# Input rows of the last two column groups loaded straight into the kept token rows, with every job and ring buffer of the first stage placed anew

## The chip, the cores and the metric

The kernel runs on one core of one Trainium2 chip. The metric is the device time of one execution in microseconds (us). A core has five engines with an instruction stream each: TensorE (PE, matmuls; PEld is its weight load), VectorE (DVE), ScalarE (ACT), GpSimd (POOL) and SyncE (SP, which here only issues DMA transfers). The streams run side by side, each in its own order, and wait for one another through semaphores. A DMA issue that has to wait holds up everything behind it in the stream that issues it.

## The reference

A block of 2048 tokens with 640 columns: a layer norm with modulation, a state-space convolution over the sequence per column, a second norm, and a bilinear gated network, each with a gated residual. Cut to what matters:

```python
mod = (silu(c) @ w_mod).reshape(1, 6, 1, -1)          # sa, ca, ga, sb, cb, gb
h = layernorm(x) * (1 + ca) + sa
K = einsum("dn,dnl,dn->dl", C, exp(dt * A * l), dt * B).real   # a filter of 2048 taps per column
y = irfft(rfft(pad(h)) * rfft(pad(K)))[:L] + h * Dskip
x = x + ga * y
h = layernorm(x) * (1 + cb) + sb
x = x + gb * (((h @ w_gate) * (h @ w_up)) @ w_down)
```

All is computed in float32; the large products of the second stage are split into high and low parts in a reduced format and summed from three products.

## The kernel before

**First stage, the convolution (about the first 465 us).** The 640 columns are five groups of 128 (`db` = 0 to 4), the tokens are four blocks of 512 (`c` or `q` = 0 to 3). The filter of each column is generated in 40 pieces (`n`), each in three parts: ACT takes sines, POOL forms phases and exponentials, DVE multiplies them (QtA, PtA, PtB, QtB), PE sums them into the bank `kg` (L825, L840). Around this loop of 144 steps lie the other jobs, each a Python generator that is emitted in segments:

- `u_stats`, `u_hm`: row statistics and normalised rows, stored to `hm`;
- `u_modr`, `u_fold`: modulation vectors on PE, folded on DVE (L392 to L404);
- `u_seeds`: the start values of each group's filter;
- `u_k`, `u_pre`, `u_g`, `u_c`: transforms of filter and rows, their product (DVE L946 to L956), and the way back, whose result goes to `WD` (store L972; by SP during the filter loop, by ACT behind it);
- `u_d(db, c)`: the end of a column group for a token block. It loads its part of `WD` (L980, into a buffer `TVa` or `TVb`) and the input rows (L982, into `xsa` or `xsb`), sums on PE (L988), adds the input rows on DVE (L992 or L995) and stores to `x2d` (L996).

**The order.** It is written out: the table `SCHED` holds a number for every segment of every job, and `due` emits a segment when the loop reaches that number (20 units are one step of the loop, two calls of `due`). Engines then run in this order. A second table, `SLOT`, names for each use of a ring buffer the letter (`a`, `b`, `c`) that it takes; a use waits until the last user of that letter is done.

**The kept rows.** The second stage begins with token blocks 0 and 1, whose rows stay in SBUF as `XB[0]`, `XB[1]` (`xb0`, `xb1`), in memory that the filter's pools give up after the last filter piece. Columns of groups 0 to 2 are read back from `x2d` (`rows`, L1384). For groups 3 and 4 (`db >= NB - 2`) and blocks 0 and 1 (`c < 2`) `u_d` writes its sum straight to `XB` (L992) and stores it to `x2d` as well, where it is read later for the residual.

**Change-over.** The last jobs are `u_d(3, 2)` and `u_d(3, 3)`, then `u_d(4, c)` in the order 0, 3, 1, 2, with `u_d(0, 2)` before the last. `warm` (L1196) puts 30 and then 4 filler matmuls on PE. `u_head` takes statistics of block 0 (L1156), normalises and transposes it (L1186) and begins the first products (L1223) as soon as `u_d(4, 0)` is done; block 1 follows after `u_d(4, 1)`. While this goes on, weight tiles (`wga`, L1021) are loaded by SP and split.

**Second stage (505 us to the end).** The gated network, half of the tokens at a time, on PE almost without a gap.

Of the kernel before, what the change touches and what calls it, by code (L numbers as in the profile page):

```python
# [14 lines left out]
OP = mybir.AluOpType  # L15
# [3 lines left out]
P = 128  # L19
# [12 lines left out]
    ml=(47, -888, -934),  # L32
    mr=(((138, 140), (110, 111)), ((2, 74), (4, 83)), ((0, 27), (-862, 18))),
    st=(
        (48, 91),
        (69, 100),
        (71, 101),
        (-948, 5),
        (-1006, 0),
        (-965, 89),  # L40
        (-1010, -969),
        (-868, 34),
        (-938, -874),
        (-918, 0),
        (-1003, -929),
        (-947, -909),
        (-919, -868),
        (34, 63),
        (37, 69),
        (-912, 0),  # L50
    ),
    hm=(
        (10, 220),
        (302, 416),
        (-1002, 172),
        (-999, 389),
        (-1010, 182),
        (-961, 147),
        (59, 100),
        (123, 173),  # L60
        (246, 310),
        (290, 372),
        (162, 252),
        (121, 180),
        (210, 293),
        (297, 381),
        (391, 486),
        (473, 556),
    ),
    rstd=(124, 87),  # L70
    tab=(367, 828),
    fo=(162, 162, 208, 238),
    e0=(4, 158),
    ds=(483, 468, 275, 262),
    mc=((87, 192, 194, 200, 210), (153, 286, 303, 326, 337), (270, 359, 369)),
    q=(
# [4 lines left out]
    ),  # L81
    pre=(
# [5 lines left out]
    ),  # L88
    c=(
# [4 lines left out]
        (  # L94
            (2433, 2608, 2608, 2648, 2679, 2703),
            (2425, 2484, 2537, 2554, 2645, 2677),
            (2477, 2493, 2636, 2656, 2680, 2719),
            (2387, 2439, 2532, 2545, 2620, 2633),
# [8 lines left out]
    ),  # L107
    k=(
        (392, 464),
        (371, 384),  # L110
        (474, 512),
        (494, 503),
        (622, 637),
        (592, 599),
        (710, 710),
        (607, 639),
        (640, 677),
        (652, 660),
        (831, 865),
        (797, 803),  # L120
        (973, 990),
        (941, 961),
        (1060, 1060),
        (1060, 1060),
        (1125, 1152),
        (1353, 1363),
        (1274, 1275),
        (1390, 1425),
        (1482, 1495),
        (1506, 1519),  # L130
        (1576, 1590),
        (1524, 1542),
        (1757, 1758),
        (1791, 1791),
        (1747, 1747),
        (1720, 1720),
        (2005, 2019),
        (1893, 1909),
        (2048, 2049),
        (2020, 2031),  # L140
        (2083, 2095),
        (2218, 2252),
        (2287, 2298),
        (2350, 2355),
        (2328, 2328),
        (2344, 2352),
        (2461, 2497),
        (2497, 2510),
    ),
    low=(168, 419, 677, 899, 1101, 1385, 1631, 1857, 2075),  # L150
    w=(2478, 2613, 2684, 2668, 2879, 2879),
    wl=(2590, 2441),
    wm=(2732, 2755),
    h=(2709, 2738, 2775, 2811, 2843, 2843, 2857, 2875),
    g=(
# [1736 lines left out]
```

## Time and profile before

| What | Value |
|---|---|
| median of three runs | 964.95 us |
| lowest and highest | 959.68, 966.23 us |
| the profiled execution, its own time | 962.34 us |
| its span, first to last instruction | 960.6 us |
| mean granted TensorE clock in it | 0.989 |
| DMA: read and written in HBM | 124.22 MB, 62.59 MB |

All readings come from the one profiled execution; its time is 1.74 us over its span and 2.61 us under the median. In rows of the timeline the first number is the start in us from the span's beginning, the second the duration, then the engine (with a q behind its name: a DMA issue in that engine's stream), the line of the kernel, the operation, written tile <- read tiles, and in brackets the idle time before it and what ended it. Ring letters stand at the end of a tile's name (`TVa`, `xsb`).

### The profile page before, as it was taken

What the parts mean: (1) busy time and instruction counts of PE and PEld (TensorE: products, weight loads), DVE (VectorE), ACT (ScalarE), POOL (GpSimd) and SP (SyncE); (2) the same over time, 40 slices, a digit from 0 to 9 for tenths busy, and PEclk for the clock granted to TensorE, in tenths of its full rate; (3) what the DMA queues carried; (4) which work ended last, traced back from release to release, by engine and by line L of the source; (5) the groups of instructions that cost most, each with busy time, mean ns of one, the idle gap of its engine ahead of it and who ended that gap; (6) DMA issues with size and microseconds to landing.
All of it is one profiled execution on the core that took longest, in us unless ns stands there. A gap on an engine that the chain in (4) does not pass through costs nothing.

```text
span 960.6 us, 27559 instructions
## 1 busy us (share of the span) xinstructions
PE 892.6 (93%) x11646; PEld 734.0 (76%) x11646; DVE 705.6 (73%) x1250; ACT 580.5 (60%) x1016; POOL 471.2 (49%) x369
## 2 busy tenths in 40 slices
PE   1898787999899899998889999999999999999998
PEld 1675555878776677887558888889999788888997
DVE  8977888878888986767688555557585766569952
ACT  6989999887988977763276333234463543435430
POOL 3998997986699668750041345320013323231110
PEclk9989999999999999999999999999999999999999
DMA  7876546435267646547894675435536576758875
GB/s 238 324 243 242 186 131 199 146 108 153 78 207 197 187 124 194 184 128 228 277 308 152 192 246 192 165 140 172 200 120 196 171 238 208 244 172 289 253 231 189
DMA packets 158819, 188.59 MB, mean 196 GB/s; under 512 B 9828, under 2 KB 128360, under 8 KB 157544
## 3 DMA queue, kind: packets, MB, share of 16 engines
q1 hardware_dynamic: 149480, 155.51, 50.3%
q0 software_dynamic: 4752, 21.63, 7.8%
q10 hardware_dynamic: 4464, 9.70, 2.7%
q8 instruction: 91, 1.49, 0.6%
q14 instruction: 32, 0.26, 0.1%
HBM read 124.22 MB, written 62.59 MB: 194 GB/s over the span
## 4 chain that ended last, share of the span: by engine, by line
PE 61%; ACT 12%; issue 10%; DVE 7%; POOL 5%; DMA 4%; SPq 0%; POOLq 0%; DVEq 0%; ACTq 0%
PE pa L1095 19%; PE psg L1095 9%; PE pa L1527 7%; PE kg L825 3%; PE kg L840 2%; PE psfa L907 2%; PE psfb L967 2%; PE psfb L907 2%; ACT L235 2%; PE psfc L967 1%; PE psfc L907 1%; PE psfa L967 1%; PE psfc L886 1%; ACT trb L235 1%; ACT tra L235 1%
## 5 line engine op out<-in xcount | busy, mean ns | idle before, releaser
L1072 POOL TENSOR_TENSOR tf<-wur,wgb 128x256 f32<-128x256 f32 x23 | 17.5, 760 | 241.5 <-DVE wtl L1043 193.2
L729 POOL TENSOR_TENSOR EQ<-LQ,RH 128x1536 f32<-128x1536 f32 x40 | 114.8, 2870 | 5.3 <-DVE QtB L785 5.3
L1043 DVE TENSOR_TENSOR wtl<-tf,wth 128x256 fp32r<-128x256 f32 (+1 forms) x72 | 37.0, 516 | 59.2 <-ACT wth L235 59.2
L729 POOL TENSOR_TENSOR Phb<-LH,DH 128x1536 int32<-128x1536 int32 x21 | 60.3, 2871 | 32.6 <-ACT trb L235 19.3
L729 POOL TENSOR_TENSOR EP<-LP,RH 128x768 f32<-128x768 f32 x40 | 61.9, 1547 | 1.7 <-ACT RH L235 1.7
L729 POOL TENSOR_TENSOR Pha<-LH,DH 128x1536 int32<-128x1536 int32 (+1 forms) x20 | 54.1, 2703 | 9.2 <-ACT trb L235 8.5
L1527 PE MATMUL pa<-wsg,sh 128*128 128x384 f32 (+1 forms) x304 | 58.1, 309 | 0.0
L840 PEld LDWEIGHTS kg<-QtB,PtB 64*32 64x32 f32 x2560 | 38.3, 108 | 13.4 <-issue 6.9
L1043 DVE TENSOR_TENSOR wsg<-wga,wsg 128x640 fp32r<-128x640 f32 x36 | 35.5, 988 | 14.8 <-ACT wsg L235 14.8
L840 PE MATMUL kg<-QtB,PtB 64*32 64x64 f32 x2560 | 44.6, 219 | 1.8 <-DVE QtB L785 1.8
L1527 PEld LDWEIGHTS pa<-wsg,sh 128*128 128x128 f32 x304 | 45.4, 188 | 0.0
L1566 POOL DMA_DIRECT2D wsg<-wdc x21 | 11.2, 532 | 66.6 <-PE pa L1579 35.7
L235 ACT ACTIVATE sh<-a 128x512 fp32r<-128x512 f32 x55 | 33.3, 626 | 13.9 <-PE psg L1579 6.2
L1043 DVE TENSOR_TENSOR sl<-a,sh 128x512 fp32r<-128x512 f32 x55 | 38.0, 710 | 3.9 <-ACT sh L235 3.9
L235 ACT ACTIVATE wsg<-wga 128x640 fp32r<-128x640 f32 x36 | 26.2, 731 | 23.7 <-PE pa L1527 12.6
L1095 PE MATMUL pa<-hh,wsg 128*128 128x512 f32 x150 | 40.0, 393 | 0.0
L235 ACT ACTIVATE a<-pa 128x512 f32<-128x512 f32 x12 | 7.2, 596 | 49.9 <-PE pa L1095 49.9
L235 ACT ACTIVATE s<-pa 128x512 f32<-128x512 f32 x12 | 7.2, 598 | 49.2 <-PE pa L1095 47.0
L235 ACT ACT_TABLE_LOAD x25 | 32.1, 1283 | 7.2 <-DMA pta<-A_A_re 4.2
L784 DVE TENSOR_TENSOR QtA<-trb,EQ 128x1024 f32<-128x1024 f32 x22 | 26.8, 1216 | 11.9 <-POOL EQ L729 4.4
L235 ACT ACTIVATE wth<-tf 128x256 fp32r<-128x256 f32 (+1 forms) x72 | 32.4, 481 | 4.5 <-DVE tf L1073 1.8
L1527 PE MATMUL pa<-wsg,sl 128*128 128x384 f32 (+1 forms) x152 | 34.5, 308 | 0.0
(672 smaller groups left out, 3230.0 us busy)
## 6 DMA issues: line engine op xcount, KB each, us to landing
wsg<-wdc POOLq DMA_DIRECT2D x21, 640.0 KB, 5.1
wgb<-B_w_gate SPq DMA_DIRECT2D x24, 320.0 KB, 4.1
wur<-B_w_up SPq DMA_DIRECT2D x24, 320.0 KB, 5.6
wsd<-wsg SPq DMA_DIRECT2D x12, 640.0 KB, 3.7
wga<-wdg SPq DMA_DIRECT2D x12, 640.0 KB, 3.9
wsg<-wsd POOLq DMA_DIRECT2D x12, 640.0 KB, 4.8
wdc<-xb SPq DMA_DIRECT2D x21, 320.0 KB, 4.5
TVb<-WD SPq DMA_DIRECT2D x26, 256.0 KB, 3.5
```

Source lines behind the costliest of these rows:

```text
L235: return S.activation(o, i, f, **kw)
L729: G.tensor_tensor(o.rearrange("p x (h l) -> p x h l", l=8), lo.unsqueeze(2).to_broadcast([P, rows, nh, 8]), hi.unsqueeze(3).to_broadcast([ ...
L784: return [lambda: V.tensor_tensor(Qt[:, :, :, 0:32], tr[:, :, :, ::-1], e[:, :, 0:32].unsqueeze(1).to_broadcast([P, 2, R, 32]), op=OP.mult ...
L825: PE.matmul(kg[j * 32 : j * 32 + 32, dd, :], PtA[:, c, dl * 4 + j, :], QtA[:, c, dl * 4 + j, :], start=dd == 0 and c == 0, stop=False, til ...
L840: PE.matmul(kg[j * 32 : j * 32 + 32, dd, :], PtB[lo : lo + 64, c, r, :], QtB[lo : lo + 64, c, r, :], start=False, stop=dd == 7 and c == 1, ...
L907: PE.matmul(r[c][par * 64 : par * 64 + 64, i, :], t_tw[:, k0 + k, c, :], src[:, k, :], start=True, stop=True, tile_position=(0, par * 64))
L967: PE.matmul(r[par][:, i], t_ti[lo : lo + 64, qd * 4 + i, c, :], y[lo : lo + 64, i, :], start=k == 0, stop=k == len(x) - 1, tile_position=( ...
L1043: V.tensor_tensor(lo, v, hi, op=OP.subtract)
L1072: E.tensor_tensor(t[:, 0:2], u[:, 0:2], g[:, 0:2], op=OP.subtract)
L1095: PE.matmul(ps, w[a][:, k], x[b][:, l], start=first and n == 0 and m == 0, stop=n == 2 and m == len(ks) - 1, skip_group_check=True)
L1527: PE.matmul(AC[tb][t][c], x[:, ts], w[:, cs], start=st, stop=f == NF - 1 and n == 2 and (c == 0 or t % 2 == 1))
L1566: G.dma_start(WD[q], wdc[:, q // 3, q % 3])
```

## The change

Four `u_d` jobs, groups 3 and 4 for blocks 0 and 1, no longer load input rows into the ring `xs`. Instead one transfer per block (`kept_l`, placed by a new entry `xl`) brings the 256 columns of both groups from the input straight to `XB[c]`, as soon as that memory is free; the add is made in place. The store to `x2d` is made once per block, of both groups together, by whichever of the two jobs comes second. The ring `xs` has 16 uses in place of 20. Every number in `SCHED` and most letters in `SLOT` are new.

```diff
 SCHED = dict(
-    ml=(47, -888, -934),
+    ml=(31, 2, -977),
...
-    fo=(162, 162, 208, 238),
+    fo=(155, 185, 229, 232),
...
-        ((2736, 2744, 2754), (2780, 2829, 2831), (2836, 2874, 2875), (2749, 2762, 2784)),
+        ((2704, 2713, 2734), (2715, 2775, 2775), (2776, 2869, 2879), (2713, 2753, 2753)),
...
+    xl=(2453, 2441),
 )
...
     def u_d(db, c):
...
-        xs = ring(fp, [P, 4, P], "xs")
-        SY.dma_start(xs, xin[:, 4 * c : 4 * c + 4, db * P : db * P + P])
-        yield
         d0 = slice(db * P, db * P + P)
+        kept = db >= NB - 2 and c < 2
+        if not kept:
+            xs = ring(fp, [P, 4, P], "xs")
+            SY.dma_start(xs, xin[:, 4 * c : 4 * c + 4, d0])
+        yield
         ps = ring(PF[-1], [P, 4, P], "psf")
...
         mark("d", c)
-        if db >= NB - 2 and c < 2:
-            V.tensor_tensor(XB[c][:, :, d0], ps, xs, op=OP.add)
+        if kept:
+            need(1, "xl", c)
             xs = XB[c][:, :, d0]
-        else:
-            V.tensor_tensor(xs, ps, xs, op=OP.add)
+        V.tensor_tensor(xs, ps, xs, op=OP.add)
+        if kept:
+            mark("kept", c)
+            if done["kept", c] < 2:
+                return
+            d0, xs = LAST, XB[c][:, :, LAST]
         SY.dma_start(x2d[:, 4 * c : 4 * c + 4, d0], xs)
...
+    LAST = slice((NB - 2) * P, NB * P)
...
+            def kept_l(tb):
+                SY.dma_start(XB[tb][:, :, LAST], xin[:, 4 * tb : 4 * tb + 4, LAST])
+                mark("xl", tb)
+
             for j in range(2):
                 XB[j] = mk(f"xb{j}", [P, 4, D])
+                at(T0["xl"][j : j + 1], once(kept_l), j)
                 at(T0["wl"][j : j + 1], once(rows), j)
```

Three places show what the new numbers do to the order. The first is SP's stream where the memory of the filter's pools comes free. `TV.. <-WD` and `xs.. <-A_u` are the loads of a `u_d`, `xb1`, `xb0` the kept rows, `gha<-FH` a load for `u_g(4, 0)`, `wga` weights of the second stage. Before:

```order
L921 DMA gha_6827<-FH_3434 128x1024
L980 DMA TVa_6849<-WD_4349 128x4x128 x2
L982 DMA xsa_6852<-A_u 128x4x128
L980 DMA TVb_7001<-WD_4349 128x4x128 x2
L982 DMA xsa_7004<-A_u 128x4x128
L1384 DMA xb1_7000<-x2d_62 128x4x384
L996 DMA x2d_62<-xb1_7000 128x4x128
L1021 DMA wga0_7060<-B_w_gate 128x5x256
L996 DMA x2d_62<-xb0_6999 128x4x128
L1384 DMA xb0_6999<-x2d_62 128x4x384
L1021 DMA wga1_7182<-B_w_gate 128x5x256
L980 DMA TVb_7247<-WD_4349 128x4x128 x2
```

And now:

```order
L981 DMA TVa_6847<-WD_4351 128x4x128 x2
L981 DMA TVb_6988<-WD_4351 128x4x128 x2
L1395 DMA xb1_7010<-A_u 128x4x256
L1395 DMA xb0_7009<-A_u 128x4x256
L922 DMA gha_7075<-FH_4018 128x1024
L1029 DMA wga0_7107<-B_w_gate 128x5x256
L981 DMA TVb_7109<-WD_4351 128x4x128 x2
L986 DMA xsb_7112<-A_u 128x4x128
L1392 DMA xb1_7010<-x2d_62 128x4x384
L1392 DMA xb0_7009<-x2d_62 128x4x384
L1029 DMA wga1_7265<-B_w_gate 128x5x256
L981 DMA TVa_7274<-WD_4351 128x4x128 x2
```

The load `gha<-FH` has moved from ahead of the group-3 jobs to behind the two new loads, two stores are gone, and the loads of `u_d(3, 2)` (the last row before; `TVb_7109`, `xsb_7112` now) stand ahead of the read-back of the kept rows.

The second place follows directly in SP's stream: the change-over. `WD_3435` before and `WD_4019` now are group 4. Before:

```order
L980 DMA TVb_7247<-WD_4349 128x4x128 x2
L982 DMA xsb_7250<-A_u 128x4x128
L980 DMA TVa_7258<-WD_4349 128x4x128 x2
L982 DMA xsa_7261<-A_u 128x4x128
L1021 DMA wga0_7266<-B_w_gate 128x5x256
L996 DMA x2d_62<-xsa_7261 128x4x128
L996 DMA x2d_62<-xsb_7250 128x4x128
L980 DMA TVb_7366<-WD_3435 128x4x128 x2
L982 DMA xsb_7369<-A_u 128x4x128
L980 DMA TVa_7410<-WD_3435 128x4x128 x2
L982 DMA xsa_7413<-A_u 128x4x128
L996 DMA x2d_62<-xb0_6999 128x4x128
```

And now:

```order
L981 DMA TVa_7274<-WD_4351 128x4x128 x2
L986 DMA xsa_7277<-A_u 128x4x128
L1029 DMA wga0_7286<-B_w_gate 128x5x256
L1003 DMA x2d_62<-xsa_7277 128x4x128
L981 DMA TVb_7363<-WD_4019 128x4x128 x2
L981 DMA TVa_7402<-WD_4019 128x4x128 x2
L986 DMA xsa_7405<-A_u 128x4x128
L981 DMA TVb_7407<-WD_4019 128x4x128 x2
L1003 DMA x2d_62<-xsb_7112 128x4x128
L1003 DMA x2d_62<-xb0_7009 128x4x256
```

The load of group 4's block 0 (`TVb_7366`, now `TVb_7363`) has one store ahead of it in place of two, and no load of input rows beside it.

The third place is DVE early in the first stage, at the end of a filter piece and the fold of the modulation (`mcol`, `dt2`, `dcol`; `PtB`, `QtB`, `QtA` are products for the filter). Before:

```order
L402 SCALAR_TENSOR_TENSOR mcol_137<-psfb_679,mcol_137 128x1
L403 TENSOR_TENSOR dt2_98<-psfb_679,dt2_98 128x4
L404 TENSOR_TENSOR dcol_138<-psfb_679,dcol_138 128x4
L810 TENSOR_TENSOR PtB_670<-trb_672,EP0_142 128x512
L784 TENSOR_TENSOR QtB_671<-trb_672,EQ0_140 128x16x32
L785 TENSOR_TENSOR QtB_671<-trb_672,EQ0_140 128x16x32
L784 TENSOR_TENSOR QtA_753<-tra_756,EQ1_141 128x32x32
```

And now:

```order
L585 TENSOR_TENSOR DH1_155<-psfc_687,shl_78 128x4x24x2
L811 TENSOR_TENSOR PtB_676<-trb_678,EP0_142 128x512
L785 TENSOR_TENSOR QtB_677<-trb_678,EQ0_140 128x16x32
L786 TENSOR_TENSOR QtB_677<-trb_678,EQ0_140 128x16x32
L393 TENSOR_SCALAR psfa_656<-psfa_656 128x5
L394 TENSOR_SCALAR mcol_137<-psfa_656 128x5
L395 TENSOR_TENSOR psfa_656<-psfa_656,mcol_137 128x5
```

The three products have moved from behind the fold's 13 small operations to ahead of them.

More of the change, by code (lines that the diff above doesn't have):

```diff
@@ L70 @@
-    rstd=(124, 87),
-    tab=(367, 828),
-    fo=(162, 162, 208, 238),
-    e0=(4, 158),
-    ds=(483, 468, 275, 262),
-    mc=((87, 192, 194, 200, 210), (153, 286, 303, 326, 337), (270, 359, 369)),
-    q=(
[4 rows of a table removed]
+    ml=(31, 2, -977),
+    mr=(((138, 143), (111, 123)), ((51, 71), (73, 90)), ((15, 18), (26, 35))),
+    st=(
+        (81, 101),
+        (90, 113),
+        (80, 115),
+        (-1010, 9),
+        (-868, 3),
+        (-908, 82),
+        (-1008, -967),
+        (6, 27),
+        (-956, -888),
+        (0, 3),
+        (-1008, -936),
+        (-965, -926),
+        (-964, 0),
+        (17, 29),
+        (30, 64),
+        (0, 7),
+    ),
@@ new lines @@
+    hm=(
+        (132, 397),
+        (444, 478),
+        (160, 173),
+        (-928, 211),
+        (110, 203),
+        (37, 155),
+        (76, 110),
+        (160, 210),
+        (230, 306),
+        (190, 299),
+        (217, 299),
+        (136, 163),
+        (314, 379),
+        (318, 379),
+        (384, 459),
+        (524, 568),
+    ),
+    rstd=(129, 84),
+    tab=(361, 785),
+    fo=(155, 185, 229, 232),
+    e0=(0, 166),
+    ds=(514, 285, 379, 342),
+    mc=((94, 198, 208, 210, 212), (178, 287, 305, 317, 338), (254, 334, 375)),
@@ L81 @@
+    q=(
[4 rows of a table added]
     ),
     pre=(
[5 rows of a table removed]
-    ),
-    c=(
[4 rows of a table removed]
-        (
[L95 to L98, printed above, removed]
[5 rows of a table added]
+    ),
+    c=(
[4 rows of a table added]
+        (
+            (2430, 2529, 2529, 2529, 2586, 2624),
+            (2426, 2426, 2487, 2494, 2584, 2621),
+            (2457, 2466, 2550, 2602, 2624, 2669),
+            (2382, 2420, 2476, 2476, 2546, 2613),
         ),
@@ L101 @@
     d=(
[5 rows of a table removed]
-    ),
-    k=(
[L109 to L148, printed above, removed]
-    ),
@@ L150 @@
[L150 to L154, printed above, removed]
-    g=(
[5 rows of a table removed]
[5 rows of a table added]
+    ),
+    k=(
+        (380, 499),
+        (365, 392),
+        (457, 508),
+        (483, 514),
+        (588, 609),
+        (574, 593),
+        (698, 706),
+        (609, 624),
+        (656, 684),
+        (664, 679),
+        (844, 868),
+        (795, 802),
+        (999, 1002),
+        (980, 980),
+        (1041, 1046),
+        (1046, 1083),
+        (1122, 1141),
+        (1341, 1341),
+        (1257, 1262),
+        (1399, 1426),
+        (1515, 1542),
+        (1484, 1498),
+        (1563, 1571),
+        (1519, 1534),
+        (1741, 1742),
+        (1780, 1789),
+        (1742, 1759),
+        (1721, 1721),
+        (2063, 2078),
+        (1896, 1917),
+        (2006, 2015),
+        (2028, 2039),
+        (2087, 2095),
+        (2200, 2229),
+        (2243, 2256),
+        (2255, 2277),
+        (2326, 2339),
+        (2349, 2360),
+        (2449, 2453),
+        (2463, 2475),
+    ),
@@ L161 @@
+    low=(173, 418, 671, 891, 1110, 1385, 1595, 1841, 2116),
+    w=(2479, 2608, 2615, 2621, 2879, 2879),
+    wl=(2556, 2523),
+    wm=(2709, 2721),
+    h=(2662, 2670, 2744, 2774, 2814, 2839, 2863, 2875),
+    g=(
[5 rows of a table added]
     ),
+    xl=(2453, 2441),
 )
 SLOT = dict(
-    Kt="abababbaabababbababa",
-    Ph="ababababababababababbbabababababaaababbb",
-    PtA="abababababababababababababababbabaababba",
-    TV="baabababaabbaabbbabbaababbaababbaabbabbaababab",
-    W="abbbbbabababbbbabbaabbaba",
-    f16="abababa",
@@ L177 @@
-    "a",
-    xs="aabababbabaaabababab",
+    Kt="abababbaabababbababb",
+    Ph="ababababababababababababababababaabababb",
+    PtA="abaaababababbbababababababababaabbababaa",
+    TV="baababaabaababababbbaabababaaababaabaaaaababab",
+    W="babaabaabaaaaabbabaabbaba",
+    f16="abababa",
+    gh="acabcacbcaccbacbcbbabcabcabccaabcabacba",
+    hf="aaccbcacbabacabcbabccabaaabbcbacaccabcabcaccabcacbabcbacbabaaacbb",
+    psf="bcbccbaaaacacbacbacabcacbbcaacbacacabcacbcbbabcabcbacbbcbcbcabcabcbaabccabacacbbacbacbacbacabababcabcabcabbcabcabcacacaa"
@@ L179 @@
+    "cbcbaacbacbacbabcabcbacacbacacbabcabcbacbbcabcbbabccbacabcbacbacbacbabaccabacbabcacbacbacababcbabccbacbacbacacabcacbcabc"
+    "acabbcabcacbacbacacbacbacbcbacabcabc",
+    tr="ababababababbbabababababababababababababababaaabababbbababababaaababababababababbbababababababababababaababbbbabababaaba"
+    "b",
+    xs="bababbababbbaaab",
 )
@@ L980, in u_d @@
             SY.dma_start(Vt[:, h], v[:, h, 4 * c : 4 * c + 4])
-        xs = ring(fp, [P, 4, P], "xs")
-        SY.dma_start(xs, xin[:, 4 * c : 4 * c + 4, db * P : db * P + P])
+        d0 = slice(db * P, db * P + P)
+        kept = db >= NB - 2 and c < 2
+        if not kept:
+            xs = ring(fp, [P, 4, P], "xs")
+            SY.dma_start(xs, xin[:, 4 * c : 4 * c + 4, d0])
         yield
-        d0 = slice(db * P, db * P + P)
         ps = ring(PF[-1], [P, 4, P], "psf")
```

39 lines of the change are left out of this document (removed), and 44 rows, old and new, of tables (c, d, g, pre).

## The prediction, made before the changed kernel ran

> **What bounds the kernel now.** I read the page first (share of each engine, then the 40 slices), then a table by stretches of the span, then the chain of work that ended last, and last the timeline of each engine between 425 and 505 us, where the edited jobs stand.
>
> ```profile
> span 960.6 us, 27559 instructions
> PE 892.6 (93%) x11646; PEld 734.0 (76%) x11646; DVE 705.6 (73%) x1250; ACT 580.5 (60%) x1016; POOL 471.2 (49%) x369
> ```
>
> The averages hide stages with different limits, so the next table cuts the span: start, three parts of the first stage, its last columns (437 to 465), the change-over to the second stage (465 to 505), and the second stage. After the two times come PE, PEld, DVE, ACT and POOL busy, then clock, DMA share and GB/s.
>
> ```profile
> 0.00:48.00 48.00, 26.14 (x275) 18.39 (x276) 43.81 (x129) 36.68 (x53) 30.73 (x37) 1.00 0.83 281
> 48.00:168.00 120.00, 99.68 (x2071) 71.77 (x2071) 98.53 (x161) 112.63 (x187) 106.82 (x67) 0.93 0.61 200
> 168.00:312.00 144.00, 138.76 (x3396) 108.95 (x3396) 119.03 (x165) 122.02 (x211) 120.62 (x69) 1.00 0.50 148
> 312.00:437.00 125.00, 118.06 (x2888) 94.99 (x2880) 98.99 (x132) 95.91 (x163) 86.86 (x46) 0.99 0.54 163
> 437.00:465.00 28.00, 23.68 (x496) 20.37 (x484) 18.74 (x39) 8.96 (x16) 0.00 (x0) 1.00 0.81 249
> 465.00:505.00 40.00, 35.54 (x180) 21.23 (x181) 30.02 (x88) 20.47 (x38) 9.78 (x15) 1.00 0.91 295
> 505.00:960.60 455.60, 450.72 (x2380) 398.28 (x2378) 296.46 (x539) 183.87 (x353) 116.43 (x138) 1.00 0.61 199
> ```
>
> From 505 us on PE is busy 450.72 of 455.60 us and the change touches nothing there: what is gained before 505 reaches the end one for one, and what is lost too. Up to 437 us the busiest engine of each stretch (DVE, ACT, PE, PE) stands idle for 4.19 + 7.37 + 5.24 + 6.94 = 23.7 us in all: no order of the same work gains more than that there. From 465 to 505 the DMA engines are busy for 0.91 of the time, and PE's 35.54 us are partly filler (30 warm-up matmuls). This is the place the edit is about.
>
> **The change-over, as it runs now.** The chain shows two loads of input rows on it:
>
> ```profile
> 461.72 7.58 DMA xsa<-A_u
> 474.75 2.96 DMA xsb<-A_u
> ```
>
> The timeline tells what they hold. First SP's issues: the eight loads of the last jobs of column group 3 and the first of group 4 (column group 4, token block 0 is the job that the second stage waits for).
>
> ```profile
> 457.34 1.02 SPq L980 DMA_DIRECT2D TVb<-WD  x2
> 458.42 0.96 SPq L982 DMA_DIRECT2D xsb<-A_u  x1
> 459.82 1.80 SPq L980 DMA_DIRECT2D TVa<-WD  x2
> 461.72 1.10 SPq L982 DMA_DIRECT2D xsa<-A_u  x1
> 472.14 0.91 SPq L980 DMA_DIRECT2D TVb<-WD  x2
> 474.75 0.37 SPq L982 DMA_DIRECT2D xsb<-A_u  x1
> ```
>
> Then PE, ACT and DVE, with what ended their idle time in brackets:
>
> ```profile
> 466.46 1.42 PE L988 MATMUL psfc<-TVa,ct 64*32 64x512 f32 x6 [1.76 <-DMA TVa<-WD]
> 469.10 7.09 PE L1196 MATMUL psg<-wsg 128*128 128x512 f32 x30
> 476.12 1.32 PE L988 MATMUL psfa<-TVb,ct 64*32 64x512 f32 x8
> 460.40 0.33 ACTq L972 DMA_DIRECT2D WD<-Wa  x1
> 466.55 0.60 ACT L235 ACTIVATE Wa<-psfb 128x512 f32<-128x512 f32 x1 [3.47 <-DMA WD<-Wa]
> 467.67 0.33 ACTq L972 DMA_DIRECT2D WD<-Wa  x1
> 477.80 0.69 DVE L992 TENSOR_TENSOR xb<-psfa,xsb 128x512 f32<-128x512 f32 x1 [0.94 <-DMA xsb<-A_u]
> ```
>
> The reader is to see that three things end close together. PE waits 1.76 us for TVa, then does the two group-3 jobs, then 30 warm-up matmuls to 476.19, and starts the job for block 0 at 476.12, with no gap. The TVb load for that job goes out at 472.14, because the last store of its data was issued at 467.67, after ACT had waited 3.47 us for the earlier store from the same buffer. And DVE's add at 477.80 waits for the input rows, though its matmul ended at 476.12 + 1.32 = 477.44. So the ring of input rows is directly worth only 0.36 us here. The 7.58 us on the chain is mostly covered: behind it stands the store (467.67 to 472.14), and behind both PE's warm-up.
>
> **The parts.** (a) The four 256 KB loads and four stores of the kept jobs become two and two of twice the size; PE's and DVE's instructions stay the same in number and shape. For the add of block 0 the wait for input rows goes: 477.80 - 477.44 = 0.36 us, bounds 0 and -0.94 (the whole idle time before it). I take -0.36.
>
> (b) The group-3 job of token block 2 is loaded before c's last jobs instead of at 457.34. Together with (a) that takes 0.5 MB (TVb and xsb) out of the queue just ahead of TVa, xsa and ACT's store. TVa's own issue does not move: it waits for the same DVE product in the same ring slot. At best TVa lands before PE is ready, which gives the 1.76 us; at worst nothing. The store that took from 460.40 to 466.5 shrinks too. How far it can is seen from one that met less traffic:
>
> ```profile
> 367.02 3.41 DMA WD<-Wb
> ```
>
> At 3.41 us it would be over before PE's results are ready at 466.46 - 1.76 = 464.7; ACT's copy then starts 1.8 us earlier, and the store, the TVb load and PE's job can follow by as much. Bounds -1.76 (PE's warm-up run is then the limit) and 0. I take -1.76, because 0.5 MB at the 295 GB/s of this stretch is 1.8 us of transfer. [...]
>
> (c) Block 1's group-3 add moves on DVE from ahead of a group-4 product to behind all of them.
>
> ```profile
> 440.50 0.69 DVE L992 TENSOR_TENSOR xb<-psfa,xsa 128x512 f32<-128x512 f32 x1 [3.52 <-PE psfa L988]
> 444.23 0.69 DVE L946 TENSOR_TENSOR TVa<-psfb,f16a 128x512 f32<-128x512 f32 x1 [0.73 <-PE psfb L907]
> 437.35 1.15 PE L907 MATMUL psfb<-f16b,t_tw 128*64 128x64 f32 x32
> 446.91 1.10 PE L907 MATMUL psfb<-f16b,t_tw 128*64 128x64 f32 x32
> ```
>
> DVE's 3.52 us wait goes, and one product starts some 2.6 us earlier. But the next one (444.23) waits for PE, which runs without a gap from 437.35 to 446.91, in the same order as after the change. Cost 0, hidden by PE; if that cover were gone it would be worth up to -2.6.
>
> (d) The two new loads wait for memory that the kernel-generation pools give up, and SP stands there until the last product has been read; behind them now stands a group-4 load (gha<-FH).
>
> ```profile
> 436.39 1.03 PE kg L840 x64
> 429.83 0.37 SPq L921 DMA_DIRECT2D gha<-FH  x1
> 449.78 0.44 PE L907 MATMUL psfc<-gha,t_tw 128*64 128x128 f32 x4 [1.55 <-DVE ghc L956]
> ```
>
> The last kernel matmul ends at 437.42, so the loads go out at about 438, and gha at about 439 instead of 429.83. PE needs it at about 448, and until 449.78 a PSUM bank would hold it anyway. In the queue are two times 512 KB and gha's 512 KB: 1.5 MB at the 249 GB/s of this stretch is 6.3 us, landing near 445.5. Cost 0, with some 4 us in hand; the upper bound is the second rival.
>
> (e) All other moves. Apart from ring letters, 24 of PE's 2918 rows, 44 of DVE's 1116, 66 of ACT's 1012 and 7 of POOL's 336 stand elsewhere; SP's are shuffled most (76 of 365). Two places show the sign.
>
> ```profile
> 57.32 0.17 DVE L392 TENSOR_SCALAR psfb<-psfb 128x5 f32<-128x5 f32 x1 [2.59 <-PE psfb L387]
> 59.31 0.69 DVE L810 TENSOR_TENSOR PtB<-trb,EP 128x512 f32<-128x512 f32 x1
> 60.51 0.68 DVE L785 TENSOR_TENSOR QtB<-trb,EQ 128x512 f32<-128x512 f32 x1
> 42.28 0.82 DVE L484 BATCH_NORM_STATS2 st<-Wb 128x6 f32<-128x320 f32 x2
> 42.45 0.20 POOL L1281 TENSOR_TENSOR ry<-rs 128x10 f32<-128x10 f32 x1 [1.67 <-DVE rs L1280]
> ```
>
> At the fold three products (59.31 to 61.19, 1.9 us) move ahead of the fold's vector work, into the 2.59 us in which DVE waits for PE: -1.9 for DVE. At 42 us the statistics of one more row (42.28, 0.82 us, with its aggregate about 1.0) move ahead of the reciprocal that POOL waits for: +1.0 for POOL. The net of the two is -0.9. The remaining moves are bounded by -23.7 (the idle time above) and, taking an equal amount of new waits, +23.7; the moved share of ACT's rows (66 of 1012) of 23.7 us is 1.5 us either way, and I take 0 for them.
>
> **Sum**, against the profiled execution's own time of 962.34 us (its span is 960.6): 962.34 - 0.36 - 1.76 + 0 + 0 - 0.9 = 959.3 us. That execution lies 2.6 us under the median of the three runs (964.95; lowest 959.68), so part of the offset returns: I forecast 960 us.
>
> **Rivals.**
> 1. The change-over doesn't shrink: TVa and the store are as late as before, since wga (640 KB) and the stores keep the DMA engines at 0.91 without the half megabyte. For it: two of the three limits must move together. Against: the 7.58 us. Time 962.34 - 0.36 - 0.9 = 961.1, or some 962 as a median.
> 2. Slower: SP held at the new loads, as in (d). It decides when gha lands after 449.78. If the two new loads took as long as the four they replace, one after another, with the median landing times of
>
> ```profile
> xsa<-A_u SPq DMA_DIRECT2D x11, 256.0 KB, 4.8
> ghc<-FH SPq DMA_DIRECT2D x6, 512.0 KB, 4.9
> ```
>
> gha would land at 438 + 4 x 4.8 + 4.9 = 462.1, which is 12.3 us late: 971.6 us. Against: loads overlap in this trace (four issued within 6 us at 457), and the new rows are twice as long.
> 3. The first stage wins back a good part of its 23.7 us idle, since most moved groups on DVE put kernel products ahead of work that can wait. A quarter of it, 6 us: 953.3 us. Against: PE's order hardly changes, PE is 96% busy from 168 to 312, and between 48 and 168 ACT and POOL pass the lead to each other, so that DVE's gains end in their queues.
>
> **How the numbers follow.** The forecast's case (change-over shrinks, rest neutral) gets 0.48, rival 1 gets 0.20, rival 3 gets 0.20, rival 2 or another loss of that kind in the moved SP queue 0.12. A measurement of this kernel can't tell changes under about 1% (9.6 us) from none; faster is under 955.3 and slower above 974.6. Rival 3 gives nearly all of faster (0.20). Rival 2 at 971.6 lies within 1%; only its worse part, with losses elsewhere in the moved SP queue, lies beyond: slower 0.08, same 0.72. The range 951 to 968 takes in the forecast's case, rival 1, most of rival 3 and the cheap half of rival 2.
>
> **What would show it.** In the profile after: no wait of the block-0 add for A_u rows; TVa's wait on PE under 1 us; the last WD store issued before 466.5 (less what the first stage shifts); the warm-up run ending where the block-0 job starts; gha landing before PE asks for it. The forecast is wrong if the second stage starts (PE's unbroken run) more than 8 us away from 505 less the shift at 437, or if the last kernel matmul moves from 437.4 by more than 6 us.

## The result: 0.6% slower, where no change or a small gain was forecast

| | before | after |
|---|---|---|
| median of 16 runs each | 962.86 us | 968.77 us |
| lowest and highest | 959.68, 968.88 | 966.58, 972.09 |
| ratio, 95% interval | | 1.0057 (1.0039 to 1.0074) |
| the profiled execution, its span | 962.34, 960.6 us | 969.30, 967.5 us |
| mean granted clock in it | 0.989 | 0.979 |

Beside later experiments the unedited changed kernel ran again: 970.02 us, 1.0088 (1.0058 to 1.0119). So by the two ratios it is slower by 5.5 to 8.5 us. Both intervals lie above 1, although the prediction held that nothing under about 1% can be told here. The time lies outside the range that was given (951 to 968), and the change has the other sign.

The page of the changed kernel:

```profile
span 967.5 us, 27557 instructions
PE 897.5 (93%) x11646; PEld 738.2 (76%) x11646; DVE 703.8 (73%) x1250; ACT 581.5 (60%) x1016; POOL 472.0 (49%) x369
```

The same stretches as in the prediction's table (two times, PE, PEld, DVE, ACT, POOL busy, clock, DMA share, GB/s):

```profile
48.00:168.00 120.00, 98.33 (x1968) 71.34 (x1966) 95.21 (x159) 109.41 (x181) 107.70 (x67) 0.90 0.61 201
168.00:312.00 144.00, 139.02 (x3307) 108.90 (x3307) 119.19 (x165) 121.87 (x210) 116.06 (x67) 0.99 0.48 141
465.00:505.00 40.00, 34.34 (x216) 21.61 (x216) 28.25 (x86) 16.96 (x31) 9.66 (x15) 0.91 0.83 253
505.00:967.50 462.50, 456.40 (x2409) 402.95 (x2407) 299.52 (x546) 190.44 (x365) 117.13 (x139) 1.00 0.61 201
```

Between 48 and 168 us ACT did 3.2 us less work in the same 120 us than before (109.41 against 112.63), at a lower PE clock (0.90, before 0.93). So time is lost there already. Three rows fix where the rest goes: the last kernel matmul, the start of the warm-up run, and the first transposes of block 1 (`pa<-ident,xb`), which open PE's unbroken run. Before, these stood at 436.39 (ending 437.42), 469.10 and 497.42. After:

```profile
441.57 1.10 PE L841 MATMUL kg<-QtB,PtB 64*32 64x64 f32 x64
474.81 7.10 PE L1204 MATMUL psg<-wsg 128*128 128x512 f32 x30
503.84 1.47 PE L1194 MATMUL pa<-ident,xb 128*128 128x128 f32 x12
```

From 437.42 to 442.67 the first stage ends 5.25 us later; from there to the warm-up 32.14 us in place of 31.68; from there to the transposes 29.03 in place of 28.32. Behind them 463.69 us against 463.15. The sum is 5.25 + 0.46 + 0.71 + 0.54 = 6.96, the difference of the profiled times.

**Where the 5.25 us come in.** Following the kernel matmuls (those that write `kg`) by their number, the two traces are 0.8 us apart at 65 us and 4.6 us at 110 us; from 126 to 437 us the distance is mostly between 4.5 and 6.6. On POOL the row that shows it is the start of the next group's phases (`D<-ptb`), which waits for a chain of small PE and ACT jobs. Before, then after:

```profile
98.05 0.74 POOL L667 TENSOR_TENSOR D<-ptb 128x96 int32<-128x96 int32 x2 [3.04 <-issue]
```

```profile
102.87 0.74 POOL L668 TENSOR_TENSOR D<-ptb 128x96 int32<-128x96 int32 x2 [2.81 <-DVE ptb L663]
```

The rows ahead of it on PE, before: the first of the fold's transposes, the row products behind them, the products of the last modulation rows.

```profile
51.95 1.27 PE L387 MATMUL psfb<-ident,TVb 1*128 1x1 f32 x10 [1.24 <-ACT TVb L235]
59.08 4.00 PE L368 MATMUL psfa<-t_ti,sil 128*128 128x384 f32 x10
82.24 1.27 PE L458 MATMUL psfa<-ident,Wb 1*128 1x1 f32 x10
86.71 4.65 PE L435 MATMUL psfa<-t_ti,sil 128*128 128x320 f32 x10 [3.20 <-DVE colT L461]
```

And after:

```profile
53.19 1.37 PE L388 MATMUL psfa<-ident,TVb 1*128 1x1 f32 x10 [2.55 <-ACT TVb L236]
58.76 1.94 PE L826 MATMUL kg<-QtA,PtAa 128*32 128x64 f32 x64
60.63 5.38 PE L369 MATMUL psfb<-t_ti,sil 128*128 128x384 f32 x10
88.92 2.26 PE L459 MATMUL psfb<-ident,Wa 1*128 1x1 f32 x10 [4.32 <-DVE RH L607]
92.97 4.04 PE L436 MATMUL psfb<-t_ti,sil 128*128 128x320 f32 x10
```

The fold starts 1.2 us later, and its row products take 1.4 us longer: 5.38 us at a mean granted clock of 0.64, in place of 4.00 us at 0.87. ACT's rows in this stretch, before:

```profile
56.38 1.04 ACT L235 ACTIVATE PtAb<-Phb 128x1024 f32<-128x1024 int32 x1
63.12 0.48 ACT L235 ACTIVATE Wb<-psfa 1x384 f32<-1x384 f32 x1 [2.93 <-PE psfa L368]
```

And after:

```profile
60.81 1.06 ACT L236 ACTIVATE PtAa<-Phb 128x1024 f32<-128x1024 int32 x1 [3.10 <-POOL LH L722]
69.42 0.37 ACT L236 ACTIVATE Wb<-psfc 1x256 f32<-1x256 f32 x1 [2.09 <-PE psfc L369]
87.80 1.28 ACT L236 ACT_TABLE_LOAD   x1
```

That table load stood at 84.40 before: 3.4 us of the 4.8 are ACT's, and 1.4 come behind it.

ACT's waits for the row products are not new: they were 2.93 and 0.57 us before and are 0.71 and 2.09 now. New is the wait of 3.10 us. The profile puts it down to POOL, but POOL's job had ended at 60.15. The job that waits writes `PtAa`, which PE's kernel matmuls, held up by the fold ahead of them, read until 60.70 (58.76 + 1.94). In `SLOT` the letters of `PtA` begin `abaaab` here and `ababab` before, so this use takes the buffer of the use just ahead of it. In all eleven profiled kernels with `abaaab` (the experiments below included) ACT starts this job 0.1 us after PE's last read of the buffer, having waited 1.66 to 4.22 us; in the nine with `ababab` it doesn't wait. Between 55 and 70 us ACT stands idle for 6.00 us in place of 4.09. With the 1.25 us that it is late at the start (`TVb`, which the fold waits for, is copied at 52.68 in place of 51.43) this is nearly the 3.4. No run changed this letter alone.

### The profile page after: what moved, and what is told of

Read it like the earlier page. It is cut to its first block, busy times and chain, and to the rows that moved or that the text cites. A ratio compares the mean times of both kernels' runs of the same rounds, so it can differ in the third digit from the quotient of the medians.

```text
span 967.5 us, 27557 instructions
## 1 busy us (share of the span) xinstructions
PE 897.5 (93%) x11646; PEld 738.2 (76%) x11646; DVE 703.8 (73%) x1250; ACT 581.5 (60%) x1016; POOL 472.0 (49%) x369
## 4 chain that ended last, share of the span: by engine, by line
PE 67%; DVE 9%; issue 9%; ACT 8%; DMA 5%; POOL 1%; SPq 0%; DVEq 0%; POOLq 0%; ACTq 0%
PE pa L1103 19%; PE psg L1103 9%; PE pa L1540 7%; PE kg L841 3%; PE kg L826 3%; PE psfb L908 2%; PE psfc L968 2%; PE psfa L908 2%; PE psfb L968 2%; PE psfc L908 2%; PE psfa L968 1%; PE psfc L887 1%; PE psfb L369 1%; DVE TVa L947 1%; PE psfa L863 1%
## 5 line engine op out<-in xcount | busy, mean ns | idle before, releaser
L730 POOL TENSOR_TENSOR Phb<-LH,DH 128x1536 int32<-128x1536 int32 x20 | 56.7, 2836 | 29.9 <-ACT tra L236 27.9
L730 POOL TENSOR_TENSOR Pha<-LH,DH 128x1536 int32<-128x1536 int32 (+1 forms) x21 | 56.9, 2710 | 8.6 <-ACT trb L236 6.4
```

What stands on the lines that cost most here:

```text
L730: G.tensor_tensor(o.rearrange("p x (h l) -> p x h l", l=8), lo.unsqueeze(2).to_broadcast([P, rows, nh, 8]), hi.unsqueeze(3).to_broadcast([ ...
```

## Experiments

Times are medians of runs, taken beside runs of the kernel before on the same chip (962.66 to 964.00 there); ratios are to it. "Tail" is the time from the last kernel matmul's end to the transposes of block 1 (before 60.00, after 61.18), "D" the start of the POOL row above. Both come from one profile of each. In kernels with an edited table the line numbers differ, since the tables are printed in fewer lines.

**1. The edit alone, twice.** The table of before, the edit, and what it needs:

```diff
-        (... (2392, 2442, 2445) ...)   # d, group 3, block 1
+        (... (2392, 2430, 2627) ...)
+    xl=(2453, 2441),
```

> The edit of the kept rows alone: all numbers and letters of the kernel before, with the new entry xl (2453, 2441), the add of column group 3 block 1 at 2627 and three PSUM letters beside it. Theory A (the loss comes from the new start-up order, the edit is a small gain): the last kernel matmul ends at 437.4 +- 0.7 us as before, and the time is 1 to 2 us under the kernel before, about 961 to 962. Rival B (the edit itself costs, by its loads or its later add): 966 or more, with the loss after 437 us. The forecast's own terms (a) and (b) would give 960.8 against 962.9.

964.44 us, ratio 1.0012 (0.9996 to 1.0027), between what the two theories expected. The first stage is nearly as before (D 98.28, the last kernel matmul ends at 438.30, 0.9 us later). In the trace the add of block 1 (455.94) had come to stand between the last two products and held the last one up by 0.6 us, so it was moved behind them (2690 in place of 2627):

> The edit alone on the table before, as in the first run, but with the add of column group 3 block 1 behind the last product in place of between the last products (there it held the last product up by 0.6 us). The edit by itself: last product 20.6 us after the last kernel matmul, warm-up at 31.7 to 32.2, the time 963.2 to 964.0, no gain on the kernel before. If the forecast's (a) and (b) were worth 2.1 us on the old table: 961.

963.93 us, 1.0013 (0.9992 to 1.0034), tail 59.40. The edit alone makes no measurable difference; its interval leaves out a gain of over 0.8 us. This prices (a) and the fewer loads and stores, but not (b): `u_d(3, 2)` keeps its old number here, so its loads still go out just ahead of TVa (`TVb` at 459.26, TVa at 461.74), and PE waits 1.67 us for TVa (before 1.76). Theory A holds for the loss (it is not the edit's), not for the gain.

**2. The start-up order put back.** In the changed kernel, all numbers and letters of the start-up jobs as before:

```diff
-    fo=(155, 185, 229, 232),
+    fo=(162, 162, 208, 238),
-    mc=((94, 198, 208, 210, 212), (178, 287, 305, 317, 338), (254, 334, 375)),
+    mc=((87, 192, 194, 200, 210), (153, 286, 303, 326, 337), (270, 359, 369)),
...
```

> The changed kernel with the numbers and ring letters of the start-up jobs (row statistics, modulation rows, fold, reciprocals, seeds of group 1, transforms of group 0, first ten filter sums) as they were before; all else as changed. Theory A (5 us are lost between 52 and 107 us, by those jobs' new places): last kernel matmul at 437.4 to 438.2 in place of 442.7, half-clock time in the first 130 us back to about 14 us, and the time about 963.5. Rival C (the loss is spread over all moved jobs, start-up is only where it shows): 442 +- 1 and 968 or more.

966.90 us, 1.0030 (1.0011 to 1.0048), against 1.0057 and 1.0088 of the changed kernel. D:

```profile
96.79 0.73 POOL L556 TENSOR_TENSOR D<-ptb 128x96 int32<-128x96 int32 x2 [3.04 <-issue]
```

So the 4.8 us at 102 us are the start-up jobs', their letters included. The rest of the expectation failed. The time is 3.4 us above the expected 963.5; half-clock time in the first 130 us is 30.7 us and not 14 (PE stood at half clock from 114.3 to 128.0 us); and the stage ended at 441.7, which is what rival C expected.

Followed by the number of the kernel matmuls, this profile is 1.3 us ahead of the kernel before at 110 us, 1.1 us behind at 168 us and 4.3 us behind at 437 us. So it loses time where other jobs were moved as well. Between 168 and 437 us the three kernels with the start-up put back (this one and two below) lose 3.2 to 5.6 us against the profile of before; the others with the rest of the changed table lose 0 to 2.4 us, and the six other kernels with the rest of the table as before (experiment 4 among them) lose at most 0.4 us. Rival C is therefore right in part: the rest of the moved jobs cost something too, or later waits hide part of what the start-up costs. Each of these numbers is from one profile, and no run put the middle of the table back, so this stays open.

**3. Half of it each.** Modulation, statistics, fold and column vectors as before, seeds and transforms as changed:

> The changed kernel with the modulation and statistics jobs as before (loads, rows, fold, reciprocals, statistics, normalised rows, column vectors), and the seeds of group 1, the first filter sums and the transforms as changed; it cuts the start-up run in two. If the late fold (1.2 us) and the column vectors behind it are the cause: 966 to 967, as the start-up run. If the order of the seeds on DVE, ACT and POOL is: 968.5 to 970.

966.08 us, 1.0042 (1.0019 to 1.0065), D 99.74; the interval overlaps that of the changed kernel's first set. Then without the fold and the column vectors:

> The changed kernel with only the first half of the start-up as before: modulation loads and rows, statistics, normalised rows, reciprocals; the fold, the column vectors, the seeds, filter sums and transforms as changed. If the loss comes from these early jobs (the fold 1.2 us late, and what follows from it): 966 to 967, as the run with all modulation and statistics jobs put back (966.1). If the column vectors' place matters most: 969 to 970.5.

970.34 us, 1.0084 (1.0067 to 1.0102), D 102.18: nothing gained. Then those two alone:

> The changed kernel with only the numbers of the fold and of the column vectors (with their last modulation rows) as before, and the PSUM letters of those uses; all statistics, rows, seeds and transforms as changed. It is the other half of the start-up run whose first half gained nothing (970.3). If this place carries the loss: 966 to 967.5. If the loss needs both halves together: 969 to 970.5.

980.30 us, 1.0187. This does not answer the question, since the mixed letters made a new wait: a ring buffer whose store was still under way.

```profile
74.49 0.48 ACT L124 ACTIVATE Wb<-psfa 1x384 f32<-1x384 f32 x1 [9.05 <-DMA hm<-Wb]
```

So the fold's and column vectors' places are needed for the gain; whether they are enough stays open. All three runs kept `abaaab`: in the first ACT still waits 2.45 us for `PtAa`, and D stays 3.0 us behind that of experiment 2, where the letter was put back with the rest. The letter is thus a rival for that part of the loss, and it was not tested.

**4. The reverse: the new start-up in the kernel before.**

> The kernel before (without the kept-row edit) with the start-up jobs' numbers and letters of the changed kernel (statistics, modulation, fold, seeds of group 1, transforms of groups 0 and 1, first ten filter sums); the reverse of the start-up run. Theory A (the start-up order costs 3 to 5 us by itself): 966 to 968, and the tail behind the last kernel matmul as before, 523.2 us. Rival C (the loss needs the rest of the new table or the edit): 963 to 964.

975.51 us, 1.0140 (1.0111 to 1.0170), D 102.45, tail 59.73. The new start-up order costs without the edit too. The 12 us are more than the changed kernel loses; in the profile 4.2 us are there at 110 us, and 7 more come in by 126 us, at the seam of the two tables, where two uses of PSUM bank b follow each other. So the size tells little beyond the 4.4 us of D.

**5. One bank letter.** The wait of 4.32 us at 88.92 looked like the cause:

```diff
-    psf="...cacbbca..."
+    psf="...cacabca..."
```

> The changed kernel with one letter changed: the PSUM bank of the ten tiny transposes that start at 88.92 us (PE waits 4.32 us there for DVE to read bank b) is a, which is free by then. Theory A1 (that wait is on the path): the transposes start near 85.2, the next row products near 90.2 in place of 92.97, the last kernel matmul at about 440 and the time about 966. Rival (ACT, whose table load ends at 89.1, sets the pace there, PE's wait is covered): last kernel matmul within 0.5 us of 442.7, time 968.5.

971.51 us, 1.0074 (1.0056 to 1.0092); no gain. The transposes did start early, and what stood behind them did not:

```profile
85.18 1.27 PE L459 MATMUL psfa<-ident,Wa 1*128 1x1 f32 x10
89.47 4.64 PE L436 MATMUL psfb<-t_ti,sil 128*128 128x320 f32 x8 [2.00 <-DVE RH L607]
102.75 0.74 POOL L668 TENSOR_TENSOR D<-ptb 128x96 int32<-128x96 int32 x2 [3.50 <-DVE ptb L663]
```

PE waited for the next bank instead (2.00 us), and ACT for a reader of bank a (0.55 us). D moved by 0.12 us. At this place the rival's reason holds: PE's longest wait was covered. The last kernel matmul ended at 447.73, though, which neither side expected.

**6. The head's buffers.** The changed table gives the second stage's first two normalised rows the same buffer, so the second waits for the first one's transposes. ACT's rows for block 0, in the changed kernel and then in the kernel before:

```profile
486.89 0.88 ACT L236 ACTIVATE hfa<-xb,hr,hr 128x128 f32<-128x128 f32 x2 [1.24 <-DVE hr L291]
488.61 0.88 ACT L236 ACTIVATE hfa<-xb,hr,hr 128x128 f32<-128x128 f32 x2 [0.84 <-PE psfa L1194]
```

```profile
481.72 0.88 ACT L235 ACTIVATE hfb<-xb,hr,hr 128x128 f32<-128x128 f32 x2 [1.24 <-DVE hr L290]
482.50 0.86 ACT L235 ACTIVATE hfc<-xb,hr,hr 128x128 f32<-128x128 f32 x2
```

```diff
-    hf="...aaacbb",
+    hf="...aacabb",
```

> The changed kernel with two letters changed: the normalised rows of the second stage's first columns take buffers a, c, a, b, b in place of a, a, c, b, b, so the second is normalised at once and not after the first was transposed. Theory (the 1.3 us lost between the block-0 add and 505 us come from that wait of 0.84 us and from the half-clock window it leads to): from block-0 add to the first x1 transposes 19.6 us in place of 20.9, time about 967.5. Rival (only the clock counts, and that window stays): the wait goes, the half-clock window stays, time 968.3 to 968.8.

969.27 us, 1.0061 (1.0042 to 1.0080): by the time alone inconclusive. The tail, which the start-up does not touch, went from 61.18 to 59.63, below the kernel before. The half-clock stretch of 6.8 us that stood at 487.7 went too (two products of the head, `psg<-hh,wsg`, took 1.20 us in it; the two at 495.43 here took 0.71), so part of this may be the clock. Put together with experiment 2:

> The changed kernel with both repairs: start-up jobs as before, and the normalised rows in buffers a, c, a, b, b. If the two add up (2.8 us by the means of the start-up run, 1.5 us by the tail of the letter run): about 964.5, between the kernel with the edit alone (964.4) and the one with the start-up alone (966.9). If the letters gain nothing in the time, as their median said: 966 to 967.

964.57 us, 1.0021 (1.0006 to 1.0036), tail 59.85 against 61.06 without the letters, D 96.54. Each repair shows in its own place; what is left to the kernel before (2 us) is near the edit alone (1.2).

**7. The clock.** Half-clock stretches (granted clock 0.50) add up to 20.5 us in the profile of before and 41.0 in that of after. That profile of before was lucky: over 103 runs of it the granted clock was 0.978 to 0.989, mean 0.984, which would be 31 us at half clock (an estimate: twice the missing share of the span); over 22 runs of the changed kernel 0.980, 39 us. Within kernels (270 runs) 1 us more at half clock goes with 0.17 us more time (correlation 0.55), so 8.5 us are worth some 1.5 us, an estimate from these runs that takes the clock for the cause, which no run shows. The edit alone (experiment 1) had 44.4 us at half clock in a profiled execution of 963.79 us, the kernel before 20.5 in one of 962.34. Two tries to act on it. First, the tiny transposes 128 columns wide:

```diff
-                PE.matmul(pc[:, m * NB + b : m * NB + b + 1], ..., ident[0:1, 0:1], ...)
+                PE.matmul(pc[:, m * NB + b : m * NB + b + P], ..., ident[0:1, 0:P], ...)
```

> The kernel before, with the 25 tiny transposes of the fold and of the column vectors 128 columns wide in place of one (the extra columns are zeros that the next one writes over), so that PE's array is no longer idle in them. Theory K (half-clock windows come from those stretches and lie on the path): no half-clock window begins at 53 to 58 us, the 30 instructions of the fold take 3.8 us in place of 5.3 and the row products behind them 3.5 in place of 4.0; last kernel matmul about 2 us earlier, time about 961. Rival (windows come from PE's waits, not from the tiny transposes, or other engines hide them): half-clock time and median as the kernel before, 963.

> The changed kernel with the same wide transposes. Theory K: of its three half-clock windows at 54.3 at most one is left; the fold takes 3.8 us in place of 5.65, the row products 3.5 in place of 5.4; the start-up ends some 3.5 us earlier and the time is about 965.3, so that the distance to the wide kernel before is near 4 us in place of 5.7. If the whole distance came from the clock, it would be the same time as the wide kernel before. Rival W (the distance comes from waits of the new order, not from the clock): gain below 1 us, about 968.

964.08 us, 1.0008 (0.9992 to 1.0025), and 971.17, 1.0084 (1.0062 to 1.0105): theory K falls. That PE's array idles in the narrow transposes was an assumption: PE is shown busy for 10.47 of 12 us with either width. The windows stayed (clock 0.72 and 0.76; 48 to 60 us, the kernel before and its wide form):

```profile
48.00:60.00 12.00, 10.47 (x165) 8.95 (x164) 9.14 (x28) 11.77 (x18) 10.48 (x14) 0.72 0.68 216
```

```profile
48.00:60.00 12.00, 10.47 (x166) 8.43 (x165) 9.76 (x29) 11.77 (x18) 10.49 (x14) 0.76 0.79 266
```

Second, the price of a window at the change-over, by leaving the 34 filler matmuls out of the kernel before:

> The kernel before without its 34 filler matmuls, so that PE idles from 469 to 476 us. It prices a half-clock window at the change-over. If such windows cost what the rows of the changed kernel suggest: one to three windows between 473 and 490 us, the first x1 transposes at 61 to 63 us after the last kernel matmul in place of 60.0, the time 1 to 3 us above the kernel before. Rival (the head waits for DVE and ACT, the clock there costs nothing): 60.0 +- 0.3 and no change.

963.43 us, 1.0006 (0.9988 to 1.0025), tail 60.75. Seventeen microseconds at half clock (22 us at a mean of 0.61),

```profile
470.00:492.00 22.00, 13.92 (x54) 5.19 (x55) 16.19 (x60) 6.47 (x13) 4.18 (x10) 0.61 0.87 265
```

cost 0.75 us: less than expected, and nothing that the time can show. The clock goes with the spread and perhaps a part of the mean; by these prices it is not the main cause.

**8. What sets TVa's landing.** The third load of weights (`wga`, 640 KB) moved behind the first kept rows' store, in both kernels:

> The changed kernel with the third load of second-stage weights (wga, 640 KB, issued at 468.12 us while PE waits for TVa) moved behind the store of block 0's kept rows. Theory (TVa's 6.85 us are set by what is in flight beside it, 2.4 MB of which this is 0.64, and not by what was ahead of it): TVa lands 1 to 1.8 us earlier, and the start of the warm-up run, counted from the last kernel matmul, comes at 30.5 to 31 us in place of 32.1; the first x1 transposes at 59.5 to 60.2 in place of 61.2. Rival (the load's own way through its queue sets it): warm-up at 32.1 +- 0.3.

> The kernel before with the third load of second-stage weights moved behind the store of block 0's kept rows, as was done with the changed kernel. If the load competes with TVa and the last store: warm-up starts at 30.9 to 31.3 us after the last kernel matmul in place of 31.7, the first x1 transposes at 59.2 to 59.6 in place of 60.0, the time about 962.3. Rival: 60.0 +- 0.2 and no gain.

970.53 us, 1.0086 (1.0062 to 1.0110), warm-up at 31.57 in place of 32.14, tail 59.94; and 965.24, 1.0022 (1.0003 to 1.0041), warm-up at 31.67 as before, tail 61.87, since the add of block 1 then waited (50.8 us after the last kernel matmul in place of 48.6). In the changed kernel the second half of TVa landed 4.89 us after its issue in place of 6.85, and PE no longer waited for it; but the last product in front of it came 0.4 us later, so only half a microsecond was left. In the kernel before, the landing did not move (6.97, before 6.99). And the kernel of experiment 5, which moves no load, shows 5.19. Whether the weights delay TVa stays open. Then the early load of `u_d(3, 2)` put back to late:

> The changed kernel with the loads of the group-3 job of block 2 (TVb and xsb, 0.5 MB) put back to behind the last products, as before the change, and the products' TV letters as before. The forecast's step (b) (that load's 0.5 MB stood ahead of TVa): putting it back costs, the warm-up run starts 1.8 us later after the last kernel matmul, 33.9 in place of 32.14. Theory H (the early load gained nothing, and by holding buffer b it made the last four products share buffer a): the last product ends at 20.6 us after the last kernel matmul in place of 21.2, and the warm-up starts at 31.6 to 32.1.

973.20 us, 1.0116 (1.0095 to 1.0136), warm-up at 37.08:

```profile
475.98 2.47 PE L879 MATMUL psfc<-TVa,ct 64*32 64x512 f32 x8 [5.04 <-DMA TVa<-WD]
```

Neither expectation fits: it cost 4.9 us, not 1.8, and gained 0.3 of the 0.6 on the products. The late load pulled the second `wga` load behind it as well (465.31 in place of 453.92), so 1.4 MB stood in front of TVa. From its first issue to the landing of its second half TVa took 9.0 us here (467.00 to 475.98), with that 1.4 MB issued in the 4 us ahead; 7.4 us in the kernel before, with 0.75 MB issued in the 2.5 us ahead; and 7.3 us in the changed kernel, with no load issued by SP in the 11 us ahead. The same move on top of experiment 6:

> Start-up as before, head letters repaired, and the group-3 job of block 2 loaded late: what is left of the change is the kept rows and the moves in the middle. If the three causes add up: 964.0 (0.6 under the run with two of them), with the last kernel matmul's own noise of +- 2 us; in no theory is it below the kernel before by more than 0.5.

971.08 us, 1.0093 (1.0059 to 1.0128), D 96.60, warm-up at 36.64: the same loss, so the sum of repairs was not tested further.

**9. The changed kernel again.**

> The changed kernel itself, unedited, beside the next three on one chip. It gives a second profile of the same program and the spread of its time. Expected 968.8 +- 1 by its own 16 runs; if the kernels made from it (971.2, 969.5, 971.4, 971.0 as means) tell of the chip and not of their edits, 970 to 971. Start-up to the last kernel matmul: if half-clock windows fall differently from run to run, it ends at another time than 442.7, anywhere from 441 to 448, with the same instructions.

970.02 us. Its second profile has the same order, D at 101.06 and the last kernel matmul's end at 443.67. In one profile each, the six kernels with the new start-up untouched have D at 101.06 to 104.16, the six with the table of before there at 98.05 to 98.39. No version beat the kernel before.

## Why the prediction was wrong, step by step

The step that failed is (e), which set the order of the first stage at nearly nothing; (b) was far too large. Of the prediction's own signs, three came true (no wait for input rows, warm-up ending where block 0's job starts, `gha` landing in time) and two did not (TVa's wait under 1 us, the last `WD` store earlier). The last kernel matmul moved by 5.25 us, inside the 6 us that it allowed.

- **(a) add of block 0, -0.36: right.** The wait for input rows is gone; the add starts as the matmul ends (481.84 + 1.09 = 482.93).

```profile
481.84 1.09 PE L991 MATMUL psfc<-TVb,ct 64*32 64x512 f32 x8
482.97 0.69 DVE L997 TENSOR_TENSOR xb<-psfc,xb 128x512 f32<-128x512 f32 x1 [1.44 <-PE psfc L991]
```

- **(b) TVa and the store earlier, -1.76: wrong, about 0.** TVa's two loads are issued from 465.68 on (23.0 us after the last kernel matmul; 22.4 before). PE starts on the first at 470.99 and on the second at 472.97, and waits 0.43 + 0.94 = 1.37 us in place of 1.76. The second load landed 6.85 us after its issue, before 6.99. ACT still waits 3.29 us for its store (before 3.47). So some 0.4 us of wait went, and the last product in front of TVa came 0.6 us later (27.88 us after the last kernel matmul in place of 27.28): the last two products share buffer `TVa` now, and where experiment 8 put their letters back it came at 27.27 in one kernel and at 27.94 in the other. Rival 1's outcome happened, not its reason: the DMA engines were busy for 0.83 between 465 and 505 us, not 0.91. What was taken out (two loads of 256 KB for TVb and one for xsb, 0.75 MB and not the 0.5 of the step) had been issued at 457.34 and 458.42; at the 257 GB/s that all DMA together moved between 457 and 460 us, the 2.5 us until TVa was issued are 0.64 MB, an estimate. That is not enough to have them landed: in the edit alone, with the same loads at the same place, the first of TVb landed 2.6 us after TVa was issued. The step took a transfer's size for its delay; why the missing transfers brought only 0.14 us stays open.

```profile
457.00:460.00 3.00, 2.44 (x44) 2.21 (x40) 2.79 (x7) 1.42 (x3) 0.00 (x0) 1.00 0.83 257
```

```profile
465.68 0.91 SPq L981 DMA_DIRECT2D TVa<-WD  x2
470.99 1.05 PE L991 MATMUL psfc<-TVa,ct 64*32 64x512 f32 x4 [0.43 <-DMA TVa<-WD]
472.97 0.62 PE L991 MATMUL psfc<-TVa,ct 64*32 64x512 f32 x2 [0.94 <-DMA TVa<-WD]
472.22 0.60 ACT L236 ACTIVATE Wa<-psfb 128x512 f32<-128x512 f32 x1 [3.29 <-DMA WD<-Wa]
```

- **(c) block 1's add, 0: right.** DVE's next product still waits for PE, now for 2.20 us.
- **(d) SP held at the new loads, 0: right.** `gha` goes out at 443.63 (1.0 us after the last kernel matmul), and PE's job on it waits for DVE as before, 1.54 us.

```profile
455.03 0.44 PE L908 MATMUL psfc<-gha,t_tw 128*64 128x128 f32 x4 [1.54 <-DVE ghc L957]
```

- **(e) all other moves, -0.9 with 1.5 either way: the step that failed.** At the place it chose, DVE's three products did move ahead of the fold (56.10 us, before 59.31). But DVE's next product came 2.0 us later (63.08, before 61.10) and not 1.9 earlier: it waits 2.14 us until ACT's `tra` is done at 62.99, and ACT had waited for `PtAa`. The fold itself, on PE, came 1.2 us later. The +1.0 on POOL did not come either (its wait for the reciprocal is 1.71 us, before 1.67). The "taken as 0" for the rest went wrong by the count: 24 of 2918 moved rows on PE and 66 of 1012 on ACT say nothing of what hangs on them. A handful, the column vectors, stand on the chain to D. And the count was made "apart from ring letters", which put the letters at nothing without a reason: those of `PtA` go with the new wait of 3.10 us, those of `TV` perhaps with 0.6 us at the change-over, and those of the head's buffers with 1.2 to 1.5 us of the tail (experiment 6). In place of -0.9 the first stage ended 5.25 us later. Experiments 2 and 4 show that the start-up jobs cost 6.1 and 4.4 us at D, 3 that part of it needs the fold's and column vectors' places; how the rest divides among jobs and letters stays open. The bounds of (e) would have held it; the 1.5 did not.
- **Not in the forecast:** the clock (some 1.5 us by correlation, experiment 7). The profile of before showed 0.93 between 48 and 168 us and the prediction didn't use it.
- **The offset:** 962.34 was called 2.6 us under the median; by 103 runs of the kernel before the median is 963.3, so the sum started about right.

In the two traces the granted clock stood at 0.50 for 6.83 us from 53.32 us on and for 3.41 us from 87.45, 111.34, 159.13 and 319.56 (before), and for 10.24 us from 54.22, for 6.83 us from 88.36, 163.45, 323.88 and 487.72, and for 3.41 us from 115.66 (after). In the 3.41 us ahead of each stretch PE is shown busy for 0.74 to 2.17 us before and for 0.00 to 1.92 after; what sets a stretch off no run shows. Its price in the kernel's time was small: 17 us cost 0.75 us at the change-over (experiment 7), and over all runs it is 0.17 us per microsecond. PE may mostly not have been what the others waited for; no run shows that either.

## What to carry to other kernels

Price a re-placed table by the chains that pass through moved rows, not by how many rows moved; above all by small jobs that hand over between several engines (here PE, ACT, DVE, POOL within 40 us). Read new ring letters as moves of their own: two neighbouring uses with one letter made a wait here (3.10 us for `PtA`, 0.84 for the head's rows), and the profile put the first down to another engine (POOL). A wait that the profile shows in front of an engine is worth nothing until the next releaser is known: removing 4.32 us gained 0.12 here. Take the clock and span of many runs before trusting one profile: the one profiled run of before was at the top of its clock range (0.989 of 0.978 to 0.989).

## What the runs showed of the hardware that was not expected

While the fold's 30 matmuls with a single contraction row ran in the kernel before (51.95 to 57.20 us), PE is shown busy for all 5.25 us, yet the mean granted clock was 0.63. In the 12 us around the fold it was 0.72 with 1 column and 0.76 with 128, PE being busy for 10.47 us in both. And the first stage ended nearly 5 us apart in profiles with the same instructions in it: the last kernel matmul ended at 442.67 and 443.67 in the changed kernel, and at 447.35 where two letters were changed that are used 40 us later (experiment 6).
